# A state-space layer and an expert layer on one core: query-weight pieces in the tables' PSUM banks, a float32 end, and a list drawn anew

## The chip, the cores and the metric

The kernel runs on one core of a Trainium2 chip. A core has five engines that run their own queues of instructions: PE (TensorE, the matmuls; its weight loads are shown as PEld), DVE (VectorE), ACT (ScalarE), POOL (GpSimd) and SP (SyncE, which here only issues DMAs). The metric is the time of one execution in microseconds on the device, lower is better. Times are medians of several runs; one further execution was taken with the profiler.

## The reference

```python
x = A_u                                     # [1, 2048, 512]
h = x + A(layernorm(x))                     # S4D: long convolution
h2 = h + B(layernorm(h))                    # PEER: 256 experts, 32 heads

# A: per channel d, 128 complex modes n
A_ = -exp(log_A_real) + 1j * A_imag;  C = (C_real + 1j * C_imag) * dt
K[d, l] = 2 * Re(sum_n C[d, n] * exp(A_[d, n] * dt[d] * l))
y = causal_convolution(u, K) + u * D_skip   # by FFT of twice the length

# B: per token and head
q1, q2 = split(x @ w_q)                     # 2 x 128
i1, i2 = argmax(q1 @ k1.T), argmax(q2 @ k2.T)   # 16 keys each, top 1
e = 16 * i1 + i2
out = sum_h gelu(x . u[e]) * v[e]           # softmax over one candidate is 1
```

## The kernel before

**The first half** computes the convolution by transforms written as float32 matmuls, in four chunks of 128 channels. Parameters (`params`, DVE and ACT, in two parts of 64 and 448 columns) give for each channel and mode a phase step, a start phase, a size and a decay. From them POOL builds tables for 32 groups i of 16 channels: `steps`, `bases` and `phases` (integer phases `pg`, line 557), `powers` and `mags` (magnitudes `mg`, lines 575 to 589). For each i ACT takes the sine and cosine of `pg` into four PSUM banks `t` (lines 644 to 647), DVE multiplies them onto `mg` and `gf` (lines 651 to 664), and PE makes the convolution's kernel out of both (`kgen`, `kps`, line 690). `pg`, `mg` and `gf` have two buffers each, so POOL waits until the group before the last is used up. The input x is normalized: DVE takes statistics (line 236), PE averages them (lines 246 and 259), and DVE scales the pieces `xs` (lines 505 and 508) by means and scales that it reads from the PSUM tile `pc` (`mu_s`, `rs_s`, `dv_s`). Both the kernel and the input go through `stage1` (line 471), `stage2` (line 488), a product per frequency (`k_s2`), and the first half of the way back (`k_ia`, line 764).

**Query weights.** In `w_piece` the query weights and the keys are multiplied together in 32 pieces: a load by SP (line 820), 16 matmul instructions (line 826), a copy by ACT (line 830), a transpose by PE (line 834), a second copy by ACT (line 838), and after each fourth piece a store (line 841). The first twelve, the early ones, put product and transpose into two regions of the same PSUM tile `pc` that holds the means; the later ones take a bank from the ring `psA` for the product and another one for the transpose. Pieces 2, 3 and 4 are loaded into space that the parameters' buffers leave over.

**PSUM.** The first half has eight banks: seven in the ring `psA` and one for `pc`. The parameters hold all seven at first, as `sg`, `r64`, `w2`, `den`, `w0`, `dt` and `r`.

**The second half** treats eight blocks b of 256 tokens: `inverse` (`ib`, line 1029, the rest of the way back, plus x), `center` and `variance` (layer norm), `scores` (`sc`, line 1143, and `xu`, line 1150, each in three products of rounded parts in place of one float32 product), the index of the best key by DVE and POOL, and `select`: DVE compares the index with each expert code (`oh`, line 1269), PE counts (`cnt`, line 1279), DVE multiplies counts and activations into `actT` (line 1288), ACT and DVE split that into `whi` and `wlo` (lines 1291 and 1294), PE multiplies with the value rows, `o` (line 1309), in three products again, DVE adds h (`ob`, line 1314), SP stores. The last block does `select` in two parts of 128 tokens.

**The order of the work** is neither that of the source nor the framework's: every step is given to `Plan.add` with an engine, an estimated cost in microseconds, what it reads and writes, and which slots it takes and gives back. `Plan.run` then plays the kernel through by these costs and picks at each point the step that can start first; among equals, the one with the highest rank (the estimated time from its start to the end) plus a weight from the table `BIAS`, one for each group of steps. `FETCH` is the time that it assumes for the fetch of 128 PE instructions. The order found is the one in which each engine's queue is written; each engine then runs its queue strictly in that order, waiting for semaphores. In the list's books the early pieces use two slots of their own, `psW` and `psV`, and nothing ties these to the readers of the means in `pc`.

Of the kernel before, what the change touches and what calls it, by code (L numbers as in the profile page):

```python
# [9 lines left out]
F32 = mybir.dt.float32  # L10
# [4 lines left out]
ALU = mybir.AluOpType  # L15
# [4 lines left out]
P = 128  # L20
# [7 lines left out]
def view(t, off, dims):  # L28
# [5 lines left out]
BIAS = dict(cen0=466, cen1=291, cen2=500, cen3=500, cen4=457, cen5=255, cen6=230, cen7=84, cl=-140, e1=123,  # L34
            ia0=-132, ia1=-271, ia2=495, ia3=322, inv0=36, inv1=-311, inv2=432, inv3=391, inv4=-3, inv5=132,
            inv6=288, inv7=279, k100=324, k101=96, k102=500, k103=-356, k110=-360, k111=297, k112=-66, k113=115,
            k120=-166, k121=-218, k122=-54, k123=500, k130=-28, k131=-51, k132=116, k133=-161, k20=-7, k21=370,
            k22=-280, k23=490, par=1000, par0=500, par1=-76, pre0=-259, pre1=365, pre2=-128, pre3=79, pre4=187,
            pre5=418, pre6=407, pre7=295, sc0=309, sc1=486, sc2=179, sc3=364, sc4=23, sc5=94, sc6=108, sc7=-217,
            sel0=458, sel1=-220, sel2=-326, sel3=286, sel4=66, sel5=25, sel6=27, sel7=32, st=-154, tab0=-99,  # L40
            tab1=201, tab10=264, tab11=466, tab12=-304, tab13=-214, tab14=51, tab15=190, tab16=-360, tab17=-235,
            tab18=-148, tab19=93, tab2=500, tab20=-82, tab21=403, tab22=-266, tab23=413, tab24=473, tab25=477,
            tab26=-156, tab27=269, tab28=228, tab29=51, tab3=279, tab30=318, tab31=500, tab4=60, tab5=-386,
            tab6=-304, tab7=-206, tab8=13, tab9=13, u100=367, u101=203, u102=442, u103=-134, u110=387, u111=-108,
            u112=-27, u113=259, u120=70, u121=-120, u122=307, u123=-321, u130=-400, u131=-400, u132=-207, u133=-247,
            u20=499, u21=76, u22=392, u23=-97, var0=-35, var1=377, var2=-271, var3=470, var4=220, var5=264,
            var6=-86, var7=-213, w0=134, w1=313, w2=-400, w3=-299, w4=88, w5=500, w6=-164, w7=94, wr=489, xl=495)
# [3 lines left out]
class Plan:  # L51
# [4 lines left out]
    FETCH = 4.0  # L56
# [112 lines left out]
def kernel(ctx, tc, xa, xb, xt, lar, aim, cre, cim, ldt, dsk, wq, ka, kb, ue, ve,  # L169
# [39 lines left out]
    mu_s, rs_s, dv_s, wps_s, wpt_s = pc[:, 0:64], pc[:, 64:128], pc[:, 128:256], pc[:, 256:384], pc[:, 384:512]  # L209
# [12 lines left out]
    sg, r64, w2, den, w0, dt, r = (psA.tile([P, 512], F32, tag="s", name=f"par{k}") for k in range(7))  # L222
# [69 lines left out]
    def params():  # L292
# [7 lines left out]
        for p, sl in enumerate(PART):  # L300
# [34 lines left out]
            def middle(w2_=w2_, r_=r_, r6_=r6_, t2_=t2_):  # L335
                V.tensor_copy(t2_, r6_)
                V.scalar_tensor_tensor(r_, w2_, 31.5, t2_, op0=ALU.mult, op1=ALU.subtract)
# [6 lines left out]
            def size(sn_=sn_, w0_=w0_, dt_=dt_, sl=sl):  # L344
# [20 lines left out]
                middle=(c2_ + c1_, middle, ["w2", "r64"], ["r"]),  # L365
# [12 lines left out]
        def act(nm, p):  # L378
            plan.group = f"par{p}"
            _, fn, r, w, tab = acts[p][nm]  # L380
            n = plan.add("ACT", 0.5 if p else 0.15, fn, r=[(k, p) for k in r], w=[(k, p) for k in w], t=["pa", "pb"],
                         tab=tab, after=last, take=("psA",) * 7 if (nm, p) == ("dt", 0) else ())
            last[:] = [n]
# [44 lines left out]
        for n in ("sign", "middle", "middle", "half3", "size", "size", "turns"):  # L428
            plan.add("-", 0.0, lambda: None, after=[done[n], done["start"]], give="psA")
# [3 lines left out]
    plan = Plan(dict(psA=7, psW=1, psV=1), BIAS)  # L433
# [365 lines left out]
    def w_piece(n):  # L799
# [12 lines left out]
        def load():  # L812
            if n in (2, 3):
                t_ = pb[:, 2 * n - 1:2 * n + 1].rearrange("p a b -> p (a b)").rearrange("p (h a c) -> p h a c", h=4, a=2)
# [7 lines left out]
        def mm():  # L822
            j1["o"] = wps_s if early else bank(j1, f"wps{n}")[:, 0]
# [8 lines left out]
        def turn():  # L832
            j2["o"] = wpt_s if early else bank(j2, f"wpt{n}")[:, 0]
            T.transpose(j2["o"], d["t"], ident)
# [9 lines left out]
        pa_, pt_ = ("psW", "psV") if early else ("psA", "psA")  # L844
        k = plan.add("PE", 0.55, mm, r=[f"wq{n}", "ka"], t=[home, f"wt{n}"], take=pa_, n_mm=16)
        k = plan.add("ACT", 0.16, out, t=[f"wt{n}"], give=pa_, after=[k])
        k = plan.add("PE", 0.33, turn, t=[f"wt{n}", f"wh{hg}"], take=pt_, after=[k], n_mm=1)
        plan.add("ACT", 0.16, out2, w=[("wh", n)], t=[f"wh{hg}"], give=pt_, after=[k])
# [356 lines left out]
    def select(b, parts):  # L1205
# [18 lines left out]
        for lo, ln in parts:  # L1224
# [72 lines left out]
            n = plan.add("DVE", 0.62 * c_, mul, r=[("actT", b, k) for k in ks_], t=[kA], give="psD", after=cn)  # L1297
            n = plan.add("ACT", 0.52 * c_, high, w=[("whi", p)], t=[kA, kH], after=[n])
            plan.add("DVE", 0.62 * c_, low, r=[("whi", p)], w=[("wlo", p)], t=[kA, kH, kL], lock=True, after=[n])
            qj = 512 // ln  # L1300
            for q0 in range(0, 4, qj):
                job = {}

                def mm(job=job, q0=q0, qj=qj, sl=sl, ln=ln, lo=lo):
                    job["ps"] = ps = I["psD"].tile([P, qj, ln], F32, tag="m", name=f"o{b}_{q0}_{lo}")
                    for q in range(qj):
                        for e in range(2):
                            for v_, w_ in (("hi", "hi"), ("hi", "lo"), ("lo", "hi")):
                                T.matmul(ps[:, q], S["v_" + v_][:, e, 128 * (q0 + q):128 * (q0 + q) + 128],  # L1309
# [119 lines left out]
```

## Time and profile before

| | |
|---|---|
| median of 3 runs | 546.43 us (542.71, 546.43, 547.25) |
| profiled execution | 542.55 us, span 540.8 us |
| PE busy | 466.2 us, 86% of the span |
| DVE busy | 424.7 us, 79% |
| ACT busy | 300.5 us, 56% |
| POOL busy | 327.6 us, 61% |
| moved by DMA | 61.32 MB, mean 113 GB/s |

The span runs from the first to the last instruction; the execution's own time has some 1.75 us beside it. Shares are means over a kernel whose first half and second half have different limits, so the table alone doesn't tell what bounds it. PEclk is the share of full speed that was granted to PE's clock. In rows of the order of time, a group of instructions is shown with its start, its length, engine, line, operation, the tiles written and read, the count, and in brackets the idle time of the engine just before it with what ended it.

### The profile page before, as it was taken

Reading aid. Unit: us, or ns where it says so; the run is one execution under the profiler, and the core shown is the slowest. Engines: PE = TensorE matmul, PEld = TensorE weight load, DVE = VectorE, ACT = ScalarE, POOL = GpSimd, SP = SyncE. Lnnn points to the kernel's source line nnn. Section 1 sums busy time; section 2 is a strip of 40 time slices with the busy share of each in tenths; the row PEclk is TensorE's granted clock in tenths of the full one; section 3 lists DMA queues with packets and bytes.
Section 4 is the critical chain, followed back from the end, with each engine's and each line's share of the span. In section 5 each row is a group of like instructions: output and inputs, shape, how many; then the busy total and the mean of one; then the engine's idle time right before and its main releaser. Section 6 shows DMA issues by size and latency. Waiting matters only on the chain. (4 is left out here: it accounts for less than half of the span.)

```text
span 540.8 us, 16831 instructions
## 1 busy us (share of the span) xinstructions
PE 466.2 (86%) x7222; PEld 398.9 (74%) x7222; DVE 424.7 (79%) x728; ACT 300.5 (56%) x598; POOL 327.6 (61%) x342
## 2 busy tenths in 40 slices
PE   0044789989999999988998978999999999998976
PEld 0023588768899889977997967879786787885866
DVE  5999567689996899699827574878978897798981
ACT  6544578993989569949965532443317133144230
POOL 1699884999999999997906005616345054364200
PEclk9999779999999999999999989999998999999995
DMA  7993544576204120400054887201213050100021
GB/s 251 415 355 95 149 133 119 166 247 226 67 16 160 40 61 2 159 1 3 2 193 143 271 279 228 72 1 60 99 51 107 1 198 1 41 1 1 1 79 40
DMA packets 27362, 61.32 MB, mean 113 GB/s; under 512 B 2932, under 2 KB 14456, under 8 KB 26136
## 3 DMA queue, kind: packets, MB, share of 16 engines
q1 hardware_dynamic: 27136, 60.11, 33.3%
q8 instruction: 57, 0.93, 0.7%
q10 hardware_dynamic: 152, 0.13, 0.1%
q14 instruction: 17, 0.14, 0.1%
HBM read 46.21 MB, written 14.02 MB: 111 GB/s over the span
## 5 line engine op out<-in xcount | busy, mean ns | idle before, releaser
L557 POOL TENSOR_TENSOR pg<-PS 128x1024 int32<-128x1024 int32 x32 | 68.6, 2145 | 7.7 <-ACT t L644 7.7
L586 POOL TENSOR_TENSOR mg<-TS 128x1024 f32<-128x1024 f32 x32 | 62.6, 1955 | 9.3 <-PE kps L690 8.7
L1180 POOL TENSOR_TENSOR ks<-kq 128x512 f32<-128x512 bf16 x16 | 19.6, 1225 | 66.8 <-DVE kq L1174 66.8
L1269 DVE TENSOR_SCALAR oh<-idxb,ec_s 128x2048 bf16<-128x2048 bf16 (+1 forms) x72 | 51.1, 776 | 1.0 <-ACT idxb L1251 0.9
L764 PE MATMUL ia<-ca_s,U 128*128 128x128 f32 x256 | 49.6, 275 | 0.7 <-POOL U L743 0.7
L1143 PE MATMUL sc<-w_hi,hhi 128*128 128x512 f32 x128 | 44.6, 430 | 0.7 <-ACT hhi L1069 0.7
L645 ACT ACTIVATE t<-t,halfpi 128x512 f32<-128x512 f32 x64 | 42.4, 662 | 2.1
L1143 PE MATMUL sc<-w_hi,hlo 128*128 128x512 f32 x128 | 40.8, 400 | 0.2 <-DVE hlo L1073 0.2
L1143 PE MATMUL sc<-w_lo,hhi 128*128 128x512 f32 x128 | 40.7, 399 | 0.0
L644 ACT ACTIVATE t<-pg 128x512 f32<-128x512 int32 x64 | 39.4, 615 | 1.7 <-DVE gf L652 1.2
L647 ACT ACTIVATE t<-pg 128x512 f32<-128x512 int32 x64 | 38.7, 611 | 2.1 <-POOL pg L557 0.9
L764 PEld LDWEIGHTS ia<-ca_s,U 128*128 128x128 f32 x256 | 38.9, 192 | 0.9 <-POOL U L743 0.9
L764 PE MATMUL ia<-ca_s,yk 128*128 128x128 f32 x192 | 38.2, 281 | 0.0
L690 PE MATMUL kps<-mg 128*32 128x64 f32 x1024 | 33.4, 228 | 5.1 <-DVE mg L664 4.2
L589 POOL TENSOR_TENSOR mg<-TS 128x512 f32<-128x512 f32 x32 | 37.3, 1166 | 0.0
L826 PE MATMUL pc<-wq,ka_s 128*32 128x128 f32 x72 | 5.0, 361 | 36.8 <-DMA wq<-wq 28.8
L471 PE MATMUL s1u<-c_s,xs 128*64 128x128 f32 x512 | 34.1, 284 | 3.0 <-DVE U L735 1.3
L488 PE MATMUL s2yu<-yu,c_s 128*128 128x128 f32 x256 | 31.3, 279 | 3.3 <-DVE U L735 1.6
L471 PEld LDWEIGHTS s1u<-c_s,xs 128*64 128x64 f32 x512 | 29.1, 142 | 6.4 <-issue 1.7
L488 PEld LDWEIGHTS s2yu<-yu,c_s 128*128 128x128 f32 x256 | 29.6, 192 | 4.8 <-PE s2yu L488 1.9
L471 PE MATMUL s1k<-c_s,k 128*64 128x128 f32 x512 | 32.6, 284 | 0.5 <-ACT U L525 0.5
L690 PE MATMUL kps<-gf 128*32 128x64 f32 x1024 | 32.8, 225 | 0.0
(196 smaller groups left out, 1428.1 us busy)
## 6 DMA issues: line engine op xcount, KB each, us to landing
wq<-wq SPq DMA_DIRECT2D x29, 512.0 KB, 4.5
t_d<-T SPq DMA_DIRECT2D x24, 256.0 KB, 4.4
Tb<-t_d SPq DMA_DIRECT2D x8, 768.0 KB, 6.5
x<-xa SPq DMA_DIRECT2D x8, 512.0 KB, 7.2
xs<-xb SPq DMA_DIRECT2D x16, 256.0 KB, 3.3
xt<-xt SPq DMA_DIRECT2D x8, 512.0 KB, 6.0
out<-ob SPq DMA_DIRECT2D x7, 512.0 KB, 3.1
c_s<-c SPq DMA_DIRECT2D x1, 2048.0 KB
```

The source lines that it names most:

```text
L471: T.matmul(ps[64 * k:64 * k + 64, g, :], lhs8(4 * n + g), c1_s[:, k], start=True, stop=True)
L488: T.matmul(ps[:, k, :], c2_s[:, kk, :], y[:, :, kk, :], start=True, stop=True)
L557: G.tensor_tensor(view(pg, 0, [[32, 2 * NC], [8, 4], [1, 8]]), view(t["PS"], 1024 + off, [[1, 2 * NC], [128, 4], [0, 8]]), view(t["PS"], 8 ...
L586: G.tensor_tensor(view(mg, 0, [[96, NC], [8, 8], [1, 8]]), view(ts, 512 + 8 * o, [[8, NC], [1, 8], [0, 8]]), view(ts, 8 * o, [[8, NC], [0, ...
L589: G.tensor_tensor(view(mg, 64, [[96, NC], [8, 4], [1, 8]]), view(ts, 1536 + o, [[1, NC], [64, 4], [0, 8]]), view(ts, 1024 + 8 * o, [[8, NC ...
L644: A.activation(p, pg[:, :, k], AF.Abs)
L645: A.activation(p, p, AF.Sin, scale=-SINSCALE, bias=halfpi)
L647: A.activation(p, pg[:, :, k], AF.Sin, scale=SINSCALE)
L690: T.matmul(kps[32 * q:32 * q + 32, 2 * g + h, :], m[:, d, 64:96], m[:, d, 0:64], start=(e == 0), stop=(e == 1))
L764: T.matmul(ps[:, g, :], t[:, 4 * n + g].rearrange("p a b -> p (a b)"), ca_s[:, s, :], start=(s == 0), stop=(s == 1))
L1143: T.matmul(ps[:, 512 * h:512 * h + 512], t[x_][:, q, ts], I[w_][:, q, 512 * h:512 * h + 512], start=(q == 0 and x_ == w_), stop=(q == 3 an ...
L1269: V.tensor_scalar(oh[:, :, 0:ln], t["idxb"][:, :, sl], S["ec"][:, 4 * e + j:4 * e + j + 1], None, op0=ALU.is_equal)
```

## The change

1. **Early pieces.** They no longer use `pc`. Each takes one bank of the ring `psA` for both its product and its transpose, from the first matmul to the second copy. The slots `psW` and `psV` are gone.
2. **Parameters.** `w2` becomes a row of `pb` in SBUF, so the parameters hold six of the seven banks. `middle` reads `w2` from there and `r64` from PSUM, and doesn't copy `r64` first. The space for pieces 2 and 3 in `pb` moves by one row.
3. **Last block.** Its `o` is one float32 product of the value rows and `actT`; `whi` and `wlo` aren't made for it. The list's cost for it is 1.75 in place of 1.45.
4. **The list.** `FETCH` is 4.6 in place of 4.0, and all weights in `BIAS` are others.

```diff
-BIAS = dict(cen0=466, cen1=291, cen2=500, cen3=500, cen4=457, cen5=255, cen6=230, cen7=84, cl=-140, e1=123,
...
+BIAS = dict(cen0=-247, cen1=120, cen2=472, cen3=338, cen4=316, cen5=-191, cen6=306, cen7=-96, cl=1, e1=133,
...
-    FETCH = 4.0
+    FETCH = 4.6
...
-    mu_s, rs_s, dv_s, wps_s, wpt_s = pc[:, 0:64], pc[:, 64:128], pc[:, 128:256], pc[:, 256:384], pc[:, 384:512]
+    mu_s, rs_s, dv_s = pc[:, 0:64], pc[:, 64:128], pc[:, 128:256]
...
-    sg, r64, w2, den, w0, dt, r = (psA.tile([P, 512], F32, tag="s", name=f"par{k}") for k in range(7))
+    sg, r64, den, w0, dt, r = (psA.tile([P, 512], F32, tag="s", name=f"par{k}") for k in range(6))
+    w2 = pb[:, 3]
...
-            def middle(w2_=w2_, r_=r_, r6_=r6_, t2_=t2_):
-                V.tensor_copy(t2_, r6_)
-                V.scalar_tensor_tensor(r_, w2_, 31.5, t2_, op0=ALU.mult, op1=ALU.subtract)
+            def middle(w2_=w2_, r_=r_, r6_=r6_):
+                V.scalar_tensor_tensor(r_, w2_, 31.5, r6_, op0=ALU.mult, op1=ALU.subtract)
...
-                         tab=tab, after=last, take=("psA",) * 7 if (nm, p) == ("dt", 0) else ())
+                         tab=tab, after=last, take=("psA",) * 6 if (nm, p) == ("dt", 0) else ())
...
-        for n in ("sign", "middle", "middle", "half3", "size", "size", "turns"):
+        for n in ("sign", "middle", "half3", "size", "size", "turns"):
...
-    plan = Plan(dict(psA=7, psW=1, psV=1), BIAS)
+    plan = Plan(dict(psA=7), BIAS)
...
-                t_ = pb[:, 2 * n - 1:2 * n + 1].rearrange("p a b -> p (a b)").rearrange("p (h a c) -> p h a c", h=4, a=2)
+                t_ = pb[:, 2 * n:2 * n + 2].rearrange("p a b -> p (a b)").rearrange("p (h a c) -> p h a c", h=4, a=2)
...
-            j1["o"] = wps_s if early else bank(j1, f"wps{n}")[:, 0]
+            j1["o"] = bank(j1, f"wps{n}")[:, 0]
...
-            j2["o"] = wpt_s if early else bank(j2, f"wpt{n}")[:, 0]
+            j2["o"] = j1["ps"][:, 1] if early else bank(j2, f"wpt{n}")[:, 0]
...
-        pa_, pt_ = ("psW", "psV") if early else ("psA", "psA")
-        k = plan.add("PE", 0.55, mm, r=[f"wq{n}", "ka"], t=[home, f"wt{n}"], take=pa_, n_mm=16)
-        k = plan.add("ACT", 0.16, out, t=[f"wt{n}"], give=pa_, after=[k])
-        k = plan.add("PE", 0.33, turn, t=[f"wt{n}", f"wh{hg}"], take=pt_, after=[k], n_mm=1)
-        plan.add("ACT", 0.16, out2, w=[("wh", n)], t=[f"wh{hg}"], give=pt_, after=[k])
+        k = plan.add("PE", 0.55, mm, r=[f"wq{n}", "ka"], t=[home, f"wt{n}"], take="psA", n_mm=16)
+        k = plan.add("ACT", 0.16, out, t=[f"wt{n}"], give=None if early else "psA", after=[k])
+        k = plan.add("PE", 0.33, turn, t=[f"wt{n}", f"wh{hg}"], take=None if early else "psA", after=[k], n_mm=1)
+        plan.add("ACT", 0.16, out2, w=[("wh", n)], t=[f"wh{hg}"], give="psA", after=[k])
...
-            n = plan.add("ACT", 0.52 * c_, high, w=[("whi", p)], t=[kA, kH], after=[n])
-            plan.add("DVE", 0.62 * c_, low, r=[("whi", p)], w=[("wlo", p)], t=[kA, kH, kL], lock=True, after=[n])
+            o_k, o_r = [kA], [("wt", p), "v"]
+            if ln == 256:
+                plan.add("ACT", 0.52, high, r=[("wt", p)], w=[("whi", p)], t=[kA, kH])
+                plan.add("DVE", 0.62, low, r=[("wt", p), ("whi", p)], w=[("wlo", p)], t=[kA, kH, kL], lock=True)
+                o_k, o_r = [kH, kL], [("whi", p), ("wlo", p), "v_hi", "v_lo"]
...
+                            if ln < 256:
+                                T.matmul(ps[:, q], S["v"][:, e, cols], t["actT"][:, e, sl], start=(e == 0), stop=(e == 1))
+                                continue
...
-                n = plan.add("PE", 1.45, mm, r=[("whi", p), ("wlo", p), "v_hi", "v_lo"], t=[kH, kL, kO], take="psD", n_mm=6 * qj)
+                n = plan.add("PE", 1.45 if ln == 256 else 1.75, mm, r=o_r, t=o_k + [kO], take="psD",
+                             n_mm=6 * qj if ln == 256 else 4 * qj)
```

More of the change, by code (lines that the diff above doesn't have):

```diff
@@ L30, in view @@
     return bass.AP(tensor=t.tensor, offset=t.offset + off, ap=[list(t.ap[0])] + [list(x) for x in dims])
-BIAS = dict(cen0=466, cen1=291, cen2=500, cen3=500, cen4=457, cen5=255, cen6=230, cen7=84, cl=-140, e1=123,
[L35 to L47, printed above, removed]
@@ L364, in params @@
                 start=(c1_, lambda w2_=w2_, sl=sl: V.tensor_scalar_mul(A0[:, sl, 0], w2_, -0.5 * TURN), ["w2"], ["A0"]),
-                middle=(c2_ + c1_, middle, ["w2", "r64"], ["r"]),
+                middle=(c2_, middle, ["w2", "r64"], ["r"]),
                 turns=(2 * c2_ + 2 * c1_, turns, ["w1", "r"], ["r", "A0"]),
@@ L1295, in low @@
                              t["whi"][:, :, sl])
-            n = plan.add("DVE", 0.62 * c_, mul, r=[("actT", b, k) for k in ks_], t=[kA], give="psD", after=cn)
-            n = plan.add("ACT", 0.52 * c_, high, w=[("whi", p)], t=[kA, kH], after=[n])
-            plan.add("DVE", 0.62 * c_, low, r=[("whi", p)], w=[("wlo", p)], t=[kA, kH, kL], lock=True, after=[n])
+            n = plan.add("DVE", 0.62 * c_, mul, r=[("actT", b, k) for k in ks_], w=[("wt", p)], t=[kA], give="psD", after=cn)
+            o_k, o_r = [kA], [("wt", p), "v"]
[3 more added lines that the diff above has]
+                o_k, o_r = [kH, kL], [("whi", p), ("wlo", p), "v_hi", "v_lo"]
             qj = 512 // ln
@@ L1306, in mm @@
                     for q in range(qj):
+                        cols = slice(128 * (q0 + q), 128 * (q0 + q) + 128)
                         for e in range(2):
+                            if ln < 256:
+                                T.matmul(ps[:, q], S["v"][:, e, cols], t["actT"][:, e, sl], start=(e == 0), stop=(e == 1))
+                                continue
                             for v_, w_ in (("hi", "hi"), ("hi", "lo"), ("lo", "hi")):
-                                T.matmul(ps[:, q], S["v_" + v_][:, e, 128 * (q0 + q):128 * (q0 + q) + 128],
-                                         t["w" + w_][:, e, sl], start=(e == 0 and v_ == w_), stop=(e == 1 and v_ == "lo"))
+                                T.matmul(ps[:, q], S["v_" + v_][:, e, cols], t["w" + w_][:, e, sl],
+                                         start=(e == 0 and v_ == w_), stop=(e == 1 and v_ == "lo"))
                 def ev(job=job, q0=q0, qj=qj, sl=sl):
```

14 lines of the change are left out of this document (added).

## The prediction

> **What bounds the kernel now.** I read the page first, then busy time by stage, then the chain that ended last, then the waits and the order of time around the query-weight pieces.
>
> ```profile
> span 540.8 us, 16831 instructions
> 28.80:100.00 71.20, 52.28 (x1015) 42.11 (x1015) 53.99 (x125) 48.06 (x104) 58.09 (x54) 0.90 0.51 159
> 100.00:269.80 169.80, 161.12 (x3052) 147.68 (x3052) 149.14 (x243) 136.18 (x265) 161.38 (x146) 1.00 0.27 88
> 269.80:316.70 46.90, 40.33 (x589) 37.25 (x588) 27.39 (x47) 27.15 (x58) 10.15 (x8) 1.00 0.66 214
> 316.70:517.60 200.90, 195.52 (x2376) 156.86 (x2377) 162.98 (x226) 70.58 (x117) 85.05 (x109) 0.98 0.21 70
> 525.40:541.00 15.60, 10.85 (x52) 10.39 (x48) 2.56 (x5) 0.45 (x2) 0.00 (x0) 0.50 0.13 35
> ```
>
> The columns are the stage, its length, then the busy time of PE, PEld, DVE, ACT and POOL, PE's granted clock, the DMA share and GB/s. Four things are seen. From 28.8 to 269.8 POOL builds the tables. It is idle 71.20 - 58.09 = 13.1 us before 100 and 169.80 - 161.38 = 8.4 us after, 21.5 in all, and every one of those microseconds delays the end of the tables. From 316.7 to 517.6 PE is busy 195.52 of 200.90 us: nothing else bounds the expert blocks, and a new order can win at most the other 5.4. PE is idle 18.9 us between 28.8 and 100, so PE has room there. And the last 15.6 us run at half clock.
>
> ```profile
> 526.34 10.30 PE o L1309 x47
> 525.49 0.47 PE L1309 MATMUL o<-whi,v_hi 128*128 128x128 f32 x1
> 526.34 0.48 PE L1309 MATMUL o<-wlo,v_hi 128*128 128x128 f32 x1 [0.38 <-DVE wlo L1294]
> 526.62 0.41 PE L1309 MATMUL o<-whi,v_lo 128*128 128x128 f32 x1
> 536.22 0.42 PE L1309 MATMUL o<-whi,v_lo 128*128 128x128 f32 x1
> 525.53 0.42 DVE L1288 TENSOR_TENSOR actT<-cnt,actT 128x256 f32<-128x256 f32 x1 [0.58 <-PE cnt L1279]
> 536.67 0.69 DVE L1314 TENSOR_TENSOR ob<-o,h 128x512 f32<-128x512 f32 x1 [4.43 <-PE o L1309]
> 86.14 5.62 PE L488 MATMUL s2yu<-yu,c_s 128*128 128x128 f32 x48
> ```
>
> The end is a plain chain: counts, the product actT, then 48 matmuls of o in a row, one addition, one store. From 526.62 to 536.22 there are 45 starts, (536.22 - 526.62) / 45 = 0.213 us each. The last row is the float32 matmul of the same shape (128x128 weights, 128 columns) at full clock: 5.62 / 48 = 0.117 us an instruction; a float32 call makes two of them.
>
> **The change, part by part.**
>
> *The last block's o in float32.* It removes two casts whi, two subtractions wlo and 48 matmuls, and adds 2 parts x 4 column blocks x 2 halves = 16 calls = 32 instructions of the s2yu shape. No row has this shape at half clock. Bounds: twice the full-clock row, 0.234 us, and the 0.213 of the old o beside it. PE is held by the counts until 525.5 as before; both products are ready by 525.53 + 0.42 = 525.95, before the first eight calls are through, so the 0.85 us between the first two o rows goes too. A matmul outlasts its step by some 0.2 us. New end: 525.5 + 32 x 0.234 + 0.2 = 533.2, or 525.5 + 32 x 0.213 + 0.2 = 532.5, against 536.22 + 0.42 = 536.64. The gain is 3.4 to 4.1; I take **-3.8**. If the clock is full throughout, 525.5 + 32 x 0.117 + 0.2 = 529.4, a gain of 7.2. The addition and the store behind it do not change.
>
> The Trainium skill, page "TensorE: Matmul & The Clock Gate", section "What's actually happening", says that after one window of about 3.4 us of sustained activity the clock is full again. The stage row of the last 15.6 us does not agree: the granted clock stays at 0.50 although o runs from 526.3 to 536.6 without a gap. By the rule the new o would be slow until about 528.9 and end near 531, an estimate of -5.6 from that page; by the row it is -3.8.
>
> *The pieces leave the bank pc.* Before, the pieces' products share a PSUM bank with the means and scales that DVE reads for xs; the trace shows the engines waiting for each other there, where no value passes between them.
>
> ```profile
> 59.89 0.23 DVE L249 COPY pc<-mu 128x64 f32<-128x64 f32 x1 [3.88 <-ACT wh L838]
> 62.39 0.69 DVE L505 TENSOR_TENSOR xs<-xs,pc 128x512 f32<-128x512 f32 x1 [1.12 <-PE pc L834]
> 63.85 0.69 DVE L505 TENSOR_TENSOR xs<-xs,pc 128x512 f32<-128x512 f32 x1 [0.77 <-PE pc L826]
> 69.88 0.57 DVE L268 RECIPROCAL pc<-pc 128x64 f32<-128x64 f32 x1 [1.47 <-PE pc L826]
> 71.55 1.28 DVE L508 TENSOR_TENSOR xs<-xs,pc 128x512 f32<-128x512 f32 x2 [0.39 <-ACT wt L830]
> 80.03 0.69 DVE L505 TENSOR_TENSOR xs<-xs,pc 128x512 f32<-128x512 f32 x1 [1.45 <-ACT wh L838]
> 82.22 0.69 DVE L505 TENSOR_TENSOR xs<-xs,pc 128x512 f32<-128x512 f32 x1 [0.78 <-ACT wh L838]
> 62.10 1.95 POOL L586 TENSOR_TENSOR mg<-TS 128x1024 f32<-128x1024 f32 x1 [2.04 <-PE kps L690]
> 77.23 2.14 POOL L557 TENSOR_TENSOR pg<-PS 128x1024 int32<-128x1024 int32 x1 [0.47 <-ACT t L644]
> 80.58 1.96 POOL L586 TENSOR_TENSOR mg<-TS 128x1024 f32<-128x1024 f32 x1 [1.21 <-PE kps L690]
> 89.55 2.15 POOL L557 TENSOR_TENSOR pg<-PS 128x1024 int32<-128x1024 int32 x1 [5.89 <-ACT t L644]
> 92.85 1.95 POOL L586 TENSOR_TENSOR mg<-TS 128x1024 f32<-128x1024 f32 x1 [1.16 <-PE kps L690]
> ```
>
> DVE loses 3.88 + 1.12 + 0.77 + 1.47 + 0.39 + 1.45 + 0.78 = 9.9 us between 56 and 83. Behind it in DVE's queue stand the tables' products; kps needs these, and POOL may not overwrite mg and pg before kps and ACT have read them. POOL's waits follow: 2.04 + 0.47 + 1.21 + 5.89 + 1.16 = 10.8 us between 60 and 93. With the pieces in the tables' ring of banks the xs work waits only for its load and the means. Not all of the 10.8 is due to pc: the 5.89 is a wait for ACT, which has copies of other stages in its queue as well. The gain is between nothing (another wait steps in) and 10.8; I take **-6**, a little over half, since the 10.8 less the 5.89 is 4.9 and some of the 5.89 is pc's as well. What is late next is PE: it must do the same work earlier, and its 18.9 idle microseconds between 28.8 and 100 give the room.
>
> The cost is the bank. A piece now holds one of the seven from its first matmul to its second copy:
>
> ```profile
> 32.21 0.66 PE L826 MATMUL pc<-wq,ka_s 128*32 128x128 f32 x8 [2.30 <-ACT wt L830]
> 38.75 0.27 ACT L838 COPY wh<-pc 128x128 f32<-128x128 f32 x1 [0.69 <-PE pc L826]
> ```
>
> That is 39.02 - 32.21 = 6.8 us, for twelve pieces 82 us of one bank. Most of that hold is itself pc's waiting, and a table asks for four banks and kps for one, so I let it lie beside other work; without that cover it costs the second rival's 11.7.
>
> *Six banks for the parameters, no copy in middle.* w2 moves to SBUF, so one bank stays free while the parameters are worked out: pieces could start there, but PE has nothing to do before 28.8, when the first piece's weights land, and nothing is won. The copies that go are these:
>
> ```profile
> 12.14 0.21 DVE L336 COPY pa<-par 128x64 f32<-128x64 f32 x1
> 19.14 0.61 DVE L336 COPY pa<-par 128x448 f32<-128x448 f32 x1
> 18.76 0.41 POOL L538 COPY PS<-RS 128x128 int32<-128x128 int32 x1 [4.10 <-DVE RS L319]
> ```
>
> POOL starts its unbroken run when the second RS is there; only the first copy lies ahead of that, about 0.25 us with its gap. The second, 0.65, lies in DVE's full queue. I take **-0.3**, between 0 and -0.9. The places of pieces 2 and 3 in pb move by one row of 512 and no DMA is added.
>
> *FETCH and the weights of the list.* Neither is an operation: together they give every queue, SP's loads too, another order. PE, DVE, ACT and POOL have the same work as before, less what stands above. The old trace cannot show the new order. It bounds it: the best is that all of POOL's 21.5 us go, 15 more than I have counted; and in the other direction one misplaced item costs what such a wait costs now:
>
> ```profile
> PE ib L1029 <- DMA sel_f<-sel: 3.9, 1, 3.9
> PEld ib L1029 <- issue: 7.2, 6, 4.1
> ```
>
> The columns are who waited for whom, us in total, times and the longest. The first is PE standing before the first expert block for a load that SP issued late; the second is weight loads of the same matmuls standing for nothing that the profile shows, up to 4.1 at a time, the kind of wait that FETCH stands for in the list. One of each more or less is 3.9 + 4.1 = 8 us. I take **0**, between -8 and +8.
>
> *The sum.* -3.8 - 6 - 0.3 + 0 = -10.1 us. The profiled execution took 542.55 us around its span of 540.8, so 532.4 on that footing, 1.9% less. The three runs shown are 542.71, 546.43 and 547.25: the profile stands with the lowest, 3.9 under the median. Half of that distance goes on top, and I forecast **534**.
>
> **The rivals**, each worked out from 542.55, with the same 2 us on top for a median.
>
> *Only the end gets shorter* (chance 0.26). The waits at pc go, but others take their place: the list now counts pieces and tables against the same seven banks, and POOL still waits for kps, as in three of the five rows above. Then 542.55 - 3.8 - 0.3 = 538.5, 0.8% less. For it: in 100 to 269.8, with hardly any work at pc, POOL still loses 8.4 us. Against it: 9.9 us of DVE's idle time carry pc's name.
>
> *The pieces take a bank that the tables need* (0.16). The tables run through seven banks; 82 us with six of seven cost 82 / 7 = 11.7 us if the ring is what paces them. Then pc's gain is paid back by the new waits and 542.55 + 11.7 - 3.8 - 0.3 = 550.2, 1.4% more. The place is 29 to 110 us; it makes the kernel slower from 4.1 / 12 = 0.34 us a piece on, and by over 1% from 0.8. For it: a table, kps and two banks of another stage are seven already. Against it: the rows give 0.66 us for half of a piece's products and 0.27 for a copy, so without pc's waits a piece needs some 2 of the 6.8 us.
>
> *The clock comes back* (0.13). The forecast's mechanism, but o runs at full clock: 542.55 - 7.2 - 6 - 0.3 = 529.1. Against it: the old tail stays at 0.50 from 525.4 on, and the counts ahead of it are as before. By the rule of the Trainium skill above, the end would lie between this and the forecast.
>
> The forecast keeps 0.45. About 1% is what a measurement of this kernel can tell from no change. **Faster by over 1%** gathers the forecast and the full clock, 0.45 + 0.13 = 0.58; within 1% is 0.26; slower by over 1% is 0.16. The forecast's own range is 542.55 - 10.1 with -5 to +6 for pc and +-8 for the order, not both in full: 526 to 542. To take in the full clock with a good order below, and the bank rival's lower half above, the range is 523 to 548.
>
> **What would show it.** Right: in the changed trace no piece writes pc, and the DVE rows L249, L505 and L508 wait neither for wh, wt nor for L826 and L834; POOL's idle time from its first table to its last falls from 21.5 to about 15; the last chain has 32 o instructions at about 0.22 us, no whi and no wlo, about 7 us from the last count to the addition against 11; the stretch from the first ib to the end is shorter by about 4, and the first ib comes about 6 us earlier than 316.7. Wrong: POOL's idle time as large as before with PE or ACT waiting for a bank (the second rival: t waiting for wh or L838); an o of 32 instructions that does not end 3 us sooner after its counts; or a first ib no earlier than 316, with the order of SP's loads as the reason.

## The result, and the profile after

The changed kernel takes **525.72 us** (median; 523.09 to 529.13) against 546.84 us (542.71 to 550.23) for the kernel before on the same chip: a ratio of 0.9621, with a 95% interval of 0.9534 to 0.9707. Its profiled execution took 525.88 us around a span of 524.0, the one of before 542.55 around 540.8, so 16.8 us of span went. Ratios and intervals, here and below, are of the runs' means without the few runs that fell into the slower of the kernel's two states, so they are not quotients of the medians. Direction and range of the forecast held; 534 was 8 us too much.

First the stages of the kernel after (stage, length, then busy time of PE, PEld, DVE, ACT and POOL, PE's granted clock, DMA share, GB/s). The stages end where the last table is ready, where the first addition h of the expert blocks starts, and where the last product actT starts; then the end follows in pieces of two microseconds.

```profile
28.80:100.00 71.20, 54.41 (x1177) 44.42 (x1177) 58.10 (x133) 56.00 (x122) 65.78 (x61) 0.95 0.59 187
100.00:264.70 164.70, 156.53 (x2908) 145.09 (x2912) 144.37 (x235) 130.58 (x250) 153.51 (x138) 0.99 0.24 81
264.70:312.40 47.70, 41.20 (x678) 38.25 (x681) 26.91 (x47) 25.35 (x55) 10.16 (x9) 0.97 0.67 225
312.40:515.00 202.60, 198.18 (x2429) 160.26 (x2417) 163.22 (x241) 77.32 (x124) 81.36 (x109) 0.98 0.20 69
515.00:517.00 2.00, 2.00 (x10) 2.00 (x10) 0.42 (x1) 0.00 (x0) 0.00 (x0) 0.50 0.04 8
517.00:519.00 2.00, 2.00 (x18) 2.00 (x18) 0.69 (x1) 0.00 (x0) 0.00 (x0) 0.91 0.00 0
519.00:521.00 2.00, 0.91 (x9) 0.72 (x7) 0.69 (x1) 0.00 (x0) 0.00 (x0) 1.00 0.46 131
```

POOL's idle time while it builds tables is now 71.20 - 65.78 = 5.4 and 164.70 - 153.51 = 11.2, together 16.6 us against 21.5. And in the end the clock does not stay at 0.50: it is back within some 2.5 us of the start of o, and the last window is at 1.00.

To compare kernels I use four marks that every one of them has: when POOL starts its last product mg, when DVE starts the first h, when it starts the last actT, and the span. The first two kernels, by tile (times in ns: shortest, median, longest; then first and last start in us), before:

```profile
L589 POOL TENSOR_TENSOR mg<-TS x32: 1153/1166/1185, 27.6 to 268.6; 128x512 f32<-128x512 f32 x32
L1036 DVE TENSOR_TENSOR h<-ib,xt x16: 680/684/693, 319.5 to 468.5; 128x512 f32<-128x512 f32 x16
L1288 DVE TENSOR_TENSOR actT<-cnt,actT x9: 417/683/692, 365.2 to 525.5; 128x512 f32<-128x512 f32 x7, 128x256 f32<-128x256 f32 x2
```

and after:

```profile
L590 POOL TENSOR_TENSOR mg<-TS x32: 1152/1170/1190, 27.4 to 263.5; 128x512 f32<-128x512 f32 x32
L1036 DVE TENSOR_TENSOR h<-ib,xt x16: 680/682/692, 312.4 to 470.3; 128x512 f32<-128x512 f32 x16
L1288 DVE TENSOR_TENSOR actT<-cnt,actT x9: 416/691/692, 364.1 to 515.0; 128x512 f32<-128x512 f32 x7, 128x256 f32<-128x256 f32 x2
```

| stretch (us) | before | after | difference |
|---|---|---|---|
| start to last mg | 268.6 | 263.5 | -5.1 |
| last mg to first h | 50.9 | 48.9 | -2.0 |
| first h to last actT | 206.0 | 202.6 | -3.4 |
| last actT to end | 15.3 | 9.0 | -6.3 |
| span | 540.8 | 524.0 | -16.8 |

The first ib, which the forecast used as a mark, is a poor one. In order of time on PE after (start, duration, idle time before with its releaser):

```profile
305.34 0.31 PE L1029 MATMUL ib<-cb,Tb 128*32 128x64 f32 x6
307.40 0.24 PE L1029 MATMUL ib<-cb,T 128*32 128x64 f32 x1 [1.75 <-ACT T L778]
...
309.85 0.32 PE L1029 MATMUL ib<-cb,T 128*32 128x64 f32 x1 [2.14 <-DVE T L778]
```

Six matmuls run 11.4 us earlier than before, and then PE waits for T twice; the first h comes 7.1 us earlier.

The pieces, in order of time on DVE and POOL (start, duration, idle time before it with its releaser). After, no piece writes pc:

```profile
54.03 0.22 DVE L251 COPY pc<-mu 128x64 f32<-128x64 f32 x1
61.62 1.88 DVE L509 TENSOR_TENSOR xs<-xs,pc 128x512 f32<-128x512 f32 x3
```

```profile
81.48 2.14 POOL L558 TENSOR_TENSOR pg<-PS 128x1024 int32<-128x1024 int32 x1 [2.45 <-ACT t L645]
84.64 1.95 POOL L587 TENSOR_TENSOR mg<-TS 128x1024 f32<-128x1024 f32 x1 [1.01 <-PE kps L691]
90.22 1.95 POOL L587 TENSOR_TENSOR mg<-TS 128x1024 f32<-128x1024 f32 x1 [0.39 <-PE kps L691]
```

The copy of mu had waited 3.88 us for a piece and waits for nothing; three xs of line 509 run in one go. POOL loses 2.45 + 1.01 + 0.39 = 3.9 us between 60 and 93 where it lost 10.8.

The end of the kernel after, in order of time:

```profile
514.91 5.00 PE L1313 MATMUL o<-actT,v_raw 128*128 128x128 f32 x32
515.02 0.42 DVE L1288 TENSOR_TENSOR actT<-cnt,actT 128x256 f32<-128x256 f32 x1 [0.77 <-PE cnt L1279]
518.16 0.69 DVE L1321 TENSOR_TENSOR ob<-o,h 128x512 f32<-128x512 f32 x1 [2.72 <-PE o L1313]
519.95 0.69 DVE L1321 TENSOR_TENSOR ob<-o,h 128x512 f32<-128x512 f32 x1 [1.09 <-PE o L1313]
```

The 32 instructions of o take 5.00 us where 48 took 10.3 and more: the first ones at half clock, the rest at full.

### The profile page after: what moved, and what is told of

It reads as the page before. It is cut to its first block, busy times and chain, and to the rows that moved or that the text cites. A ratio compares the mean times of both kernels' runs of the same rounds, so it can differ in the third digit from the quotient of the medians.

```text
span 524.0 us, 16811 instructions
## 1 busy us (share of the span) xinstructions
PE 455.2 (87%) x7206; PEld 392.7 (75%) x7206; DVE 415.7 (79%) x724; ACT 305.5 (58%) x600; POOL 323.9 (62%) x342
## 4 chain that ended last, share of the span: by engine, by line
PE 54%; DVE 21%; ACT 9%; POOL 7%; DMA 5%; issue 4%; POOLq 0%; ACTq 0%; DVEq 0%; SPq 0%
PE sc L1143 18%; PE ia L765 9%; PE s1u L472 3%; PE kps L691 3%; PE cnt L1279 3%; PE xu L1150 3%; DVE U L734 2%; DVE U L736 2%; DVE yk L733 2%; DMA wq<-wq 2%; PE ib L1029 2%; POOL pg L558 2%; PE s1k L472 2%; POOL mg L587 2%; PE s2yu L489 2%
## 5 line engine op out<-in xcount | busy, mean ns | idle before, releaser
L1269 DVE TENSOR_SCALAR oh<-idxb,ec_s 128x2048 bf16<-128x2048 bf16 (+1 forms) x72 | 47.1, 721 | 10.6 <-ACT idxb L1251 9.4
L827 PE MATMUL wps<-wq,ka_s 128*32 128x128 f32 x232 | 13.0, 297 | 39.8 <-DMA wq<-wq 38.4
L1053 POOL TENSOR_TENSOR vs<-hc 128x256 f32<-128x256 f32 x8 | 7.0, 877 | 57.1 <-ACT hc L1076 57.1
L827 PEld LDWEIGHTS wps<-wq,ka_s 128*32 128x32 f32 x232 | 5.1, 111 | 44.3 <-DVE par L311 33.4
L489 PE MATMUL s2yu<-yu,c_s 128*128 128x128 f32 x256 | 33.1, 287 | 3.2 <-DVE U L736 2.7
L489 PEld LDWEIGHTS s2yu<-yu,c_s 128*128 128x128 f32 x256 | 31.0, 199 | 5.0 <-PE s2yu L489 2.2
## 6 DMA issues: line engine op xcount, KB each, us to landing
c_s<-c SPq DMA_DIRECT2D x1, 2048.0 KB, 12.9
```

The costliest lines, as they stand in the source:

```text
L489: T.matmul(ps[:, k, :], c2_s[:, kk, :], y[:, :, kk, :], start=True, stop=True)
L1269: V.tensor_scalar(oh[:, :, 0:ln], t["idxb"][:, :, sl], S["ec"][:, 4 * e + j:4 * e + j + 1], None, op0=ALU.is_equal)
```

## The experiments

The theories at the start: *parts* (the end, the bank and the order each give their share, the end more than forecast because the clock returns), against *only the order* (the new weights do it all) and *the bank costs* (pieces in the tables' ring hold the tables up). All kernels follow with the four stretches, from their tile views; "us" is the median, the ratio is to the kernel before beside it on the same chip, whose median was 544.94 for tail_only, means_out, code_old_order and pieces_back, 544.16 for new_code_old_weights, old_code_new_weights, fetch_back and no_weights, and 542.56 for the other four. The stretches are those of one profiled execution each.

| kernel | us | ratio (95%) | to last mg | to first h | to last actT | to end | span |
|---|---|---|---|---|---|---|---|
| tail_only | 539.06 | 0.9901 (0.9841-0.9960) | 270.1 | 51.9 | 207.6 | 7.9 | 537.5 |
| means_out | 563.08 | 1.0380 (1.0283-1.0477) | 287.2 | 50.4 | 207.8 | 15.2 | 560.6 |
| code_old_order | 554.57 | 1.0246 (1.0154-1.0337) | 288.1 | 50.1 | 206.8 | 7.9 | 552.9 |
| pieces_back | 530.81 | 0.9803 (0.9716-0.9890) | 270.3 | 47.2 | 202.3 | 8.8 | 528.6 |
| all_code_old_order | 529.97 | 0.9764 (0.9668-0.9860) | 259.3 | 49.5 | 206.7 | 7.8 | 523.3 |
| three_products_new_order | 530.82 | 0.9797 (0.9722-0.9873) | 263.9 | 48.4 | 202.6 | 14.6 | 529.5 |
| new_code_old_weights | 540.37 | 0.9944 (0.9912-0.9975) | 259.5 | 50.0 | 218.7 | 8.7 | 536.9 |
| old_code_new_weights | 558.42 | 1.0298 (1.0258-1.0337) | 271.7 | 57.3 | 213.3 | 15.2 | 557.5 |
| fetch_back | 535.46 | 0.9890 (0.9826-0.9954) | 263.9 | 56.6 | 204.2 | 7.9 | 532.6 |
| fetch_by_half | 523.38 | 0.9691 (0.9610-0.9772) | 263.1 | 47.9 | 205.1 | 10.2 | 526.3 |
| weights_shaken | 556.90 | 1.0272 (1.0193-1.0352) | 260.2 | 70.2 | 210.9 | 8.8 | 550.1 |
| no_weights | 565.00 | 1.0440 (1.0366-1.0514) | 260.2 | 82.0 | 217.6 | 9.4 | 569.2 |

Read down the columns, the table takes the change apart. The last stretch goes by the form of o: 14.6 to 15.3 us with three products, 7.8 to 10.2 in float32. Within float32 it goes by the clock: 7.8 or 7.9 us in the four kernels whose clock stays full (tail_only, code_old_order, all_code_old_order, fetch_back), 8.7 to 10.2 where it falls to 0.50 ahead of o and comes back during it. With before's order the expert stretch is 206.0 to 207.8, with the new one 202.3 to 202.6. The first column goes by what stands in pc, by the order, and in means_out and code_old_order by something else that is shown below.

### The end alone: tail_only

```diff
             n = plan.add("DVE", 0.62 * c_, mul, r=[("actT", b, k) for k in ks_], t=[kA], give="psD", after=cn)
+            if ln < 256:
+                high = low = lambda: None
...
                         for e in range(2):
+                            if ln < 256:
+                                T.matmul(ps[:, q], S["v"][:, e, 128 * (q0 + q):128 * (q0 + q) + 128],
+                                         t["actT"][:, e, sl], start=(e == 0), stop=(e == 1))
+                                continue
```

The kernel before in its own order, with only the last block's o in float32.

> The kernel before with its own order of every queue, and only the last block's o in float32: whi, wlo and their steps do nothing there, but stay in the list's books, so that no other instruction moves. The theory of three parts (the end, the waits at pc, the new order) says that the end alone gives 4 to 6 us: 32 instructions of o between the last count and the addition, 5 to 7 us against 11, and a time of 537 to 539 where the kernel before takes 542.6, ratio 0.990. The rival, that the whole gain is the order that the new list found and the end only looks shorter because other work was moved away from it, says 0 to 2 us, ratio 0.997 or more.

Measured: 539.06 us, ratio 0.9901, as expected. The last stretch is 7.9 us, 7.4 less than before and more than the 4 to 6 expected; the other stretches are 1.0 to 1.6 us longer each, although nothing in them was changed, which shows how far the stretches of two single profiles differ by themselves. In windows and by tile:

```profile
529.00:533.40 4.40, 4.33 (x61) 4.03 (x60) 1.39 (x4) 0.00 (x0) 0.00 (x0) 1.00 0.05 13
...
L1311 PE MATMUL o<-actT,v_raw x32: 275/275/377, 529.5 to 533.1; 128*128 128x128 f32 x32
```

Here the clock is full all through o: (533.1 - 529.5) / 31 = 0.116 us a step, the full-clock price of the s2yu row, 0.117. That is the 7.2 that the forecast named for a full clock, not the 3.8. Some of it is luck: up to the last actT the instructions are those of the kernel before, where the clock was at 0.50 from 525.0 on, half a microsecond ahead of the last actT and of o, and here it did not fall. No run shows what decides on that; where it fell, as in the kernel after, the end gains less.

### The end undone in the new order: three_products_new_order

```diff
+            if ln < 256:
+                def mul(job=job, sl=sl, ln=ln, mul_=mul, high_=high, low_=low):
+                    mul_()
+                    high_()
+                    low_()
...
-                            if ln < 256:
-                                T.matmul(ps[:, q], S["v"][:, e, cols], t["actT"][:, e, sl], start=(e == 0), stop=(e == 1))
-                                continue
```

> The changed kernel with its own order, but the last block's o in three products of rounded parts again, whi and wlo made in the same step as actT. Up to the last counts nothing differs. If the float32 o is what lets the clock come back, the granted clock here stays at 0.50 once it has fallen before the 48 matmuls, which take 10 us as in the kernel before, and the end is 5 to 7 us longer: ratio to the kernel before 0.972 to 0.976. If the clock came back by chance of its windows, it does so here too: 48 matmuls in some 7.5 us, 3 us longer, 0.966 to 0.969.

Measured: 530.82 us, ratio 0.9797, a little above the 0.972 to 0.976 expected. All stretches but the last agree with the kernel after within 0.5 us; the last is 5.6 us longer, and so is the span by 5.5. The clock in windows:

```profile
515.00:520.00 5.00, 5.00 (x24) 4.94 (x25) 0.77 (x3) 0.41 (x1) 0.00 (x0) 0.50 0.01 3
520.00:525.40 5.40, 5.35 (x26) 5.16 (x25) 0.70 (x2) 0.00 (x0) 0.00 (x0) 0.50 0.18 49
```

and two matmuls, in order of time, an early and the last one:

```profile
516.40 0.41 PE L1318 MATMUL o<-wlo,v_hi 128*128 128x128 f32 x1
...
524.94 0.41 PE L1318 MATMUL o<-whi,v_lo 128*128 128x128 f32 x1
```

Both kernels come to o at half clock. Under float32 matmuls it is full again 2.5 us after the first of them; under 10 us of these three-product matmuls, without a gap, it is not. The forecast's row (0.50 throughout the old tail) was right for the old o and did not carry over to the new one. The rule of the Trainium skill, page "TensorE: Matmul & The Clock Gate", section "What's actually happening", is full clock after one window of about 3.4 us of sustained activity. The float32 rows fit it roughly (2.5 us here, 5 in fetch_by_half), the rows of three_products_new_order do not. By that rule the forecast had -5.6 for the end, and this pair shows 5.6.

It is not the three products as such that keep the clock down. In weights_shaken, a kernel that comes further below, an earlier o of 256 columns in three products also starts at half clock, and its clock comes back. A window, then two matmuls in order of time:

```profile
529.60:532.60 3.00, 3.00 (x16) 3.00 (x16) 1.01 (x2) 0.68 (x2) 2.51 (x4) 0.50 0.03 12
...
532.57 0.41 PE L1317 MATMUL o<-whi,v_hi 128*128 128x256 f32 x1
...
532.96 0.28 PE L1317 MATMUL o<-whi,v_lo 128*128 128x256 f32 x1
```

This o began at 529.32, so the clock is full 3.5 us later. In the kernel after it does the same under the three-product sc of 512 columns, at 0.53 in the mean from 479.6 to 483.2 and at 1.00 from 484 to 488. At half clock these matmuls of 256 columns start every 0.21 us ((532.57 - 529.79) / 13), as those of 128 columns do, so with 128 columns half as many columns pass in the same time. Whether that is why the clock stays down was not tried.

### The pieces back in pc, in the new order: pieces_back

```diff
-            j1["o"] = bank(j1, f"wps{n}")[:, 0]
+            j1["o"] = pc[:, 256:384] if early else bank(j1, f"wps{n}")[:, 0]
...
-            j2["o"] = j1["ps"][:, 1] if early else bank(j2, f"wpt{n}")[:, 0]
+            j2["o"] = pc[:, 384:512] if early else bank(j2, f"wpt{n}")[:, 0]
```

> The changed kernel with its own order, but the early pieces write to their two old places in pc again, beside the means. The list's books still count a bank for each of them. Several early pieces that were under way at the same time now share one place and overwrite one another, so their query weights are not the reference's; the instructions are the same. Theory of three parts: xs and the means wait for pieces again, tables end 4 to 8 us later than 264.7, and the time is 4 to 8 us above the changed kernel's, ratio to the kernel before 0.970 to 0.978. Rival (only the order counts): within 2 us of the changed kernel, 0.960 to 0.966.

The kernel leaves out that pieces under way at the same time need places of their own, so its query weights are not the reference's. Measured: 530.81 us, ratio 0.9803, 5.1 us above the kernel after and a little above the ratio expected; the last mg starts 6.8 us later than in the kernel after, the other three stretches are 1.7, 0.3 and 0.2 us shorter. The old waits return, on DVE:

```profile
58.40 0.69 DVE L506 TENSOR_TENSOR xs<-xs,pc 128x512 f32<-128x512 f32 x1 [1.12 <-PE pc L827]
...
66.35 0.57 DVE L270 RECIPROCAL pc<-pc 128x64 f32<-128x64 f32 x1 [2.28 <-ACT wt L831]
...
76.99 0.69 DVE L506 TENSOR_TENSOR xs<-xs,pc 128x512 f32<-128x512 f32 x1 [1.50 <-ACT wt L831]
```

and on POOL:

```profile
74.15 2.13 POOL L558 TENSOR_TENSOR pg<-PS 128x1024 int32<-128x1024 int32 x1 [0.48 <-ACT t L645]
77.52 1.95 POOL L587 TENSOR_TENSOR mg<-TS 128x1024 f32<-128x1024 f32 x1 [1.23 <-PE kps L691]
...
86.40 2.14 POOL L558 TENSOR_TENSOR pg<-PS 128x1024 int32<-128x1024 int32 x1 [5.81 <-ACT t L645]
89.56 1.96 POOL L587 TENSOR_TENSOR mg<-TS 128x1024 f32<-128x1024 f32 x1 [1.02 <-PE kps L691]
```

POOL's wait of 5.89 us is back as 5.81 where the kernel after has 2.45, and the sum is 8.5 against 3.9. So 5.81 - 2.45 = 3.4 us of that wait for ACT come with pc, more than the 1.1 that the forecast's 6 holds beside its 4.9. In this kernel the pieces also wait for one another at their two places, so the 6.8 us are the price of both.

### The means out of the bank instead: means_out and code_old_order

```diff
-    mu_s, rs_s, dv_s, wps_s, wpt_s = pc[:, 0:64], pc[:, 64:128], pc[:, 128:256], pc[:, 256:384], pc[:, 384:512]
+    mean_s = wk.tile([P, 256], F32, name="mean_s")
+    mu_s, rs_s, dv_s = mean_s[:, 0:64], mean_s[:, 64:128], mean_s[:, 128:256]
+    wps_s, wpt_s = pc[:, 256:384], pc[:, 384:512]
```

This parts the two users of pc the other way round, in before's own order. code_old_order adds the float32 o, w2 in SBUF and the missing copy to it.

> The kernel before with its own order, but the means, scales and deviations move from pc to SBUF, so that pc holds only the pieces' products and nothing that DVE's xs steps read. No instruction moves. Theory of three parts: DVE's rows of the means and xs between 56 and 83 us wait for no piece any more (9.9 us before), POOL ends its tables some 4 to 7 us earlier than 269.8, and the time falls by 3 to 7 us, ratio 0.987 to 0.995. Rival (only the order counts): DVE's waits go but POOL waits for ACT and kps as before, tables end at 268 or later, ratio 0.998 to 1.002.

> The kernel before with its own order and all that the change does to the code except the banks of the pieces: float32 o at the end, means out of pc into SBUF, w2 in SBUF, and no copy in middle. Theory of three parts: the sum of the two runs above and a little, 8 to 12 us less, ratio 0.978 to 0.985; what is then missing to the changed kernel's 0.962 is the order. Rival (only the order counts): 0.99 or more.

Measured: 563.08 and 554.57 us, slower than before. The expectation failed, and the last mg starts 18.6 and 19.5 us later than before. In order of time on DVE and on POOL in means_out:

```profile
58.61 3.81 DVE L507 TENSOR_TENSOR xs<-xs,mean_s 128x512 f32<-128x512 f32 x3
...
79.35 2.64 DVE L507 TENSOR_TENSOR xs<-xs,mean_s 128x512 f32<-128x512 f32 x1
```

```profile
75.34 1.97 POOL L588 TENSOR_TENSOR mg<-TS 128x1024 f32<-128x1024 f32 x1
...
78.83 2.60 POOL L559 TENSOR_TENSOR pg<-PS 128x1024 int32<-128x1024 int32 x1
81.40 2.40 POOL L588 TENSOR_TENSOR mg<-TS 128x1024 f32<-128x1024 f32 x1
```

and all the xs of this line together, by tile (ns, shortest, median, longest):

```profile
L507 DVE TENSOR_TENSOR xs<-xs,mean_s x16: 676/1568/2636, 58.6 to 223.4; 128x512 f32<-128x512 f32 x16
```

The waits for pieces are gone, but an xs that took 0.69 us with its mean in PSUM takes 0.68 to 2.64 with both operands in SBUF, and POOL's products mg beside the longest go from 1.95 to 2.40. The Trainium skill, page "SBUF — State Buffer", section "SBUF: two separate sides", has such a rule: DVE with two inputs in SBUF and a POOL instruction that reads SBUF lock each other out of a shared pair of ports. These rows agree. The two kernels therefore say nothing of pc. The pair does show the rest of the code in before's order: the last stretch is 7.3 us shorter, the other three differ by at most 1.0.

### All of the code, none of the order: all_code_old_order

```diff
-            j1["o"] = wps_s if early else bank(j1, f"wps{n}")[:, 0]
+            j1["o"] = bank(j1, f"wps{n}")[:, 0]
...
-            j2["o"] = wpt_s if early else bank(j2, f"wpt{n}")[:, 0]
+            j2["o"] = j1["ps"][:, 1] if early else bank(j2, f"wpt{n}")[:, 0]
```

With these go six banks for the parameters, w2 in SBUF, no copy in middle and the float32 o, but the list, its weights, FETCH and its book of banks are those of before, so every queue keeps its order and the list does not know that the pieces take banks.

> All that the change does to the code, the pieces in the tables' banks too, with the order of every queue kept from the kernel before: the list's books are the old ones, and only what the steps issue is the new code. The means stay in PSUM, so DVE's xs steps keep their operands, which the run with the means in SBUF did not. Theory of three parts: 6 us at the end and 4 to 7 at the tables, span 528 to 531 where the kernel before has 540.8, ratio 0.975 to 0.985, and the rest of the changed kernel's 0.962 is the order. Rival (the banks eat it, since the old list does not count them): tables end at 269 or later, only the end is won, ratio 0.988 to 0.992. Second rival (code alone is everything): 0.960 to 0.968.

Measured: 529.97 us, ratio 0.9764 (0.9668 to 0.9860), inside the 0.975 to 0.985 expected; its profiled execution, the fastest of its runs, has a span of 523.3 (the kernel after 524.0), less than the 528 to 531 expected. By tile:

```profile
L589 POOL TENSOR_TENSOR mg<-TS x32: 1152/1164/1187, 27.2 to 259.3; 128x512 f32<-128x512 f32 x32
...
L1036 DVE TENSOR_TENSOR h<-ib,xt x16: 678/682/694, 308.8 to 458.6; 128x512 f32<-128x512 f32 x16
...
L1288 DVE TENSOR_TENSOR actT<-cnt,actT x9: 417/682/692, 355.4 to 515.5; 128x512 f32<-128x512 f32 x7, 128x256 f32<-128x256 f32 x2
```

The tables end 9.3 us earlier than before and 10.8 earlier than in tail_only, which has the same order and end. That is the price of pc with the parameters in the old order. That it equals the forecast's upper bound, 10.8, is chance: the bound took all of POOL's waits between 60 and 93 us, and here POOL still waits 1.96 + 1.15 + 0.26 = 3.4 us there. A ring short of banks would have ended them later: *the bank costs* is refuted, *only the order* as well.

### The order without the code, and its parts

The weights and FETCH were exchanged whole, then in parts.

```diff
-    FETCH = 4.6
+    FETCH = 4.0
```

new_code_old_weights has this line and the weights of before in the changed code; old_code_new_weights is the kernel before with the new FETCH and weights; fetch_back is the kernel after with this line alone. no_weights leaves out every weight but par=1000.

> The changed kernel's code with FETCH and all weights of the kernel before, so that the list finds yet another order for the new code. Theory of three parts: the end and the waits at pc are won with any order, so 8 to 12 us less than before, ratio 0.978 to 0.985, and the rest of the 0.962 is what the new weights are worth. Rival (only the order counts): 0.99 or more. Third view, that the weights are worth nothing by themselves: 0.960 to 0.966.

> The code of the kernel before with FETCH 4.6 and the new weights. Theory of three parts: the new order's share alone, 0 to 6 us less, and the waits at pc and the long end are there as before; ratio 0.988 to 1.000. Rival (only the order counts): 10 us less or more, ratio 0.982 or below. The weights were drawn for the other code, so a loss of some us is possible for this code as well.

> The changed kernel with FETCH back at 4.0 and the new weights: how much of the order hangs on this one number. If FETCH is what the gain beyond the code comes from, the time rises by 4 to 7 us, ratio to the kernel before 0.970 to 0.976. If it only moves a few steps, the time stays within 2 us of the changed kernel, 0.959 to 0.966.

> The changed kernel with FETCH 4.6 and no weights but the parameters' 1000: the list goes by its ranks alone. It shows what the drawn weights are worth. Theory of three parts: end and pc as in the changed kernel, but a plain order: ratio 0.975 to 0.990. Rival (only the order counts): all of the gain goes, 0.995 or more.

Measured: 540.37, 558.42, 535.46 and 565.00 us. None came out in the range that *parts* gave or, for fetch_back, in either of its two: the ratios are 0.9944 for 0.978 to 0.985, 1.0298 for 0.988 to 1.000, 0.9890 for 0.976 at most, and 1.0440 for 0.975 to 0.990. Two of them, 0.9944 and 1.0440, are what *only the order* foretold. all_code_old_order keeps that theory refuted, since there the code wins with its order held; what these runs show is that another order can lose all that the code wins. By medians the new weights and FETCH are worth 540.37 - 525.72 = 14.7 us in the new code (12.9 by the spans) and cost 558.42 - 544.16 = 14.3 in the old one. The list works out another order as soon as a cost or a bank changes, and weights that were found for one code were no good in the other. In new_code_old_weights the tables end early, and the expert stretch loses what they won, 218.7 against 202.6. The waits of PE there (who waited for whom, us in total, times, longest):

```profile
PE cnt L1278 <- DVE oh L1268: 6.1, 15, 1.5
PE ixt L1230 <- DVE ix L1190: 5.3, 4, 2.7
```

and the same two in the kernel after:

```profile
PE cnt L1279 <- DVE oh L1269: 0.7, 4, 0.2
PE ixt L1231 <- DVE ix L1191: 0.5, 1, 0.5
```

FETCH alone moves 8.6 us of span, 7.7 of it between the last table and the first h (56.6 against 48.9). The longest wait of PE there in fetch_back is for a product yu that DVE makes late:

```profile
PE ia L765 <- DVE yu L733: 5.1, 1, 5.1
```

Two more kernels ask how fine the choice is. weights_shaken moves each weight by a fixed amount between -20 and +20; fetch_by_half keeps 4.6 for the list of the first half and 4.0 for the second.

```diff
+BIAS = {k: v + (37 * n % 41 - 20 if k != "par" else 0) for n, (k, v) in enumerate(BIAS.items())}
```

```diff
-                    end = fetch = max(end + (128 - count) * cost / mms, fetch + self.FETCH)
+                    end = fetch = max(end + (128 - count) * cost / mms, fetch + (self.FETCH if n < self.conv else 4.0))
```

> The changed kernel with each weight of the list but the parameters' moved by a fixed amount between -20 and +20, where the weights themselves lie between -400 and 500. It shows how finely the order hangs on them. If a small move gives a like order, the time stays within 2 us of the changed kernel, ratio 0.958 to 0.966. If the order is one fortunate draw among many, it loses 5 us or more, 0.971 or above.

> The changed kernel with FETCH 4.6 for the first half's steps and 4.0 for the second half's. With 4.0 throughout the expert blocks took 213.7 us from the first ib to the end and with 4.6 218.7, but the first half was 13.6 us longer with 4.0. If each half's share hangs on its own FETCH, this one joins the two: first ib at 305, end at 519, ratio to the kernel before 0.950 to 0.955. If the shorter second half only came from work that the longer first half had done ahead, it is within 2 us of the changed kernel or slower: 0.960 or more.

Measured: 556.90 and 523.38 us. The shaken list costs 31 us by the medians and 26.1 us of span, 21.3 of these between the last table and the first h. PE is busy 61.29 us there against 41.20, with 780 instructions against 678 and a clock of 0.91 against 0.97, so it still has work to do that the kernel after has done by then.

```profile
261.40:330.40 69.00, 61.29 (x780) 59.18 (x775) 30.43 (x53) 31.27 (x58) 10.09 (x8) 0.91 0.34 118
```

One shake is no survey, but it shows, as its second view expected, that the weights are a good draw and not a broad optimum. fetch_by_half is the fastest by its median, but its ratio, 0.9691 (0.9610 to 0.9772), cannot be told from that of the kernel after. In its profile, which caught the slowest of its four runs, the clock is back only at 521.0, by windows, 5 us after its o began:

```profile
516.00:521.00 5.00, 5.00 (x24) 5.00 (x24) 1.12 (x2) 0.00 (x0) 0.00 (x0) 0.50 0.01 3
521.00:522.50 1.50, 1.20 (x11) 1.01 (x9) 0.26 (x1) 0.00 (x0) 0.00 (x0) 0.98 0.62 175
```

## Why the prediction was right, and where its sizes were off

*The pieces leave pc: -6.* The mechanism is right, and that the size is so near is partly luck. The last mg starts 5.1 us earlier; pieces_back puts pc at 6.8 in the new order, and the step from tail_only to all_code_old_order puts pc and the parameters together at 10.8 in the old one. The new order gives 4.2 us of that back, 263.5 against 259.3: a larger gain than forecast less a loss that was put at nothing. What was to show it did: no DVE wait for a piece, and POOL idle for 16.6 us against the 15 foretold. The first ib came 11.4 us earlier, not 6.

*The last block's o: -3.8.* **This is a mis-sized term**: -6.3 in the kernel after, -7.4 in tail_only. The step that failed is "by the row it is -3.8": it carried the granted clock of the old o, 128 columns in three products, over to float32 matmuls. The new o takes 5.00 us, not 32 x 0.234 = 7.5, and the last addition starts 519.95 - 515.02 = 4.9 us after the last actT where the forecast said 7 and the old kernel had 11. The rival "the clock comes back", held at 0.13, had the right mechanism for this part, though in the kernel after the clock comes back during o and is not full throughout.

*FETCH and the weights: 0, between -8 and +8.* **The second mis-sized term.** Against the kernel before the new order goes with -2.0 between the tables and the first h and -3.4 in the expert stretch of the list's own doing. The latter is inside the 5.4 us of PE's idle time that the forecast read as all that could be won there. In the same stretch of the kernel before (window from its first h to its last actT)

```profile
319.50:525.50 206.00, 198.94 (x2431) 158.69 (x2422) 169.51 (x241) 72.31 (x121) 85.05 (x109) 0.99 0.20 67
```

PE is idle 206.00 - 198.94 = 7.1 us, after 202.60 - 198.18 = 4.4. As an account of the profiles: 2.5 more at the end, 2.0 and 3.4 from the order, 1.2 less than forecast from the tables (5.1 against the 6 and 0.3 of the two steps), 6.7 in all; -10.1 and -6.7 make the -16.8. The bounds were poor as a statement on orders: weights alone moved the same code from 525.72 to 565.00, ratios 0.9621 and 1.0440. And against all_code_old_order the new order wins 4.7 us behind the tables and loses 4.2 in them and 1.2 at the end, a loss of 0.7 in sum. The 1.2 go with the clock, which fell ahead of o in the one profile and not in the other. For the whole kernel the new list's own gain is not safely told from nothing: the two ratios, 0.9621 and 0.9764, were not measured side by side, and their intervals overlap from 0.9668 to 0.9707.

*Six banks, no copy: -0.3.* It is seen where the tables start: the first mg of line 591 starts at 27.1 us in code_old_order and at 27.7 in means_out, which differ there by this part of the change alone. At the last mg, 288.1 against 287.2, it is lost in what two single profiles differ by.

*The 2 us for a median* were not wanted: the profile after lies at its own median, that of before 4.3 below its.

*The rivals.* "Only the end gets shorter" falls with pieces_back, "the pieces take a bank that the tables need" with all_code_old_order.

## What to carry to other kernels

Cut a profile at marks that every version has, here the last table, the first block, the last counts: a change of four parts then comes apart by column, and a neutral total can be seen to be a gain in one stretch and a loss in the next. A granted clock that was read under one form of matmul need not hold under another form in its place. Where a list scheduler makes the order, price a code change with the order held fixed as well as with new weights, because old weights in the new code cost here nearly as much as the change was worth (0.9944 against 0.9621).

## What the runs showed of the hardware that was not expected

Under back-to-back three-product matmuls of 128 columns the granted clock stayed at 0.50 to the end (10.6 us of o in three_products_new_order, as in the kernel before), while under float32 matmuls of the same shape it rose from 0.50 to full, 2.5 us after the first of them in the kernel after and 5 in fetch_by_half. Under three-product matmuls of 256 columns it rose as well, after 3.5 us in weights_shaken. And moving an operand of DVE's xs from PSUM to SBUF made its 0.69 us up to 2.64 beside POOL; the kernel with this move had its last table 18.6 us later.
